# The second MLP's product block is rounded one group later, and the next tokens are transposed through four PSUM banks

## The chip, the cores and the metric

The kernel runs on one core of a Trainium2 chip. The metric is the device time of one execution in microseconds (us). Beside it, one profiled execution leaves a trace, which gives the start and length of nearly every instruction on each engine: TensorE (PE, its weight loads apart as PEld), VectorE (DVE), ScalarE (ACT), GpSimd (POOL) and the DMA queue of SyncE (SP).

## What is computed

The reference runs a linear-attention recurrence over 4 x 768 tokens, a mixture of experts over its 3072 output rows, and then a second MLP without experts. The change touches only the last stage:

```
a = x @ w1            # 3072x384 @ 384x1024
b = x @ w2
h = a * b @ w3
return (h @ w_out)    # 1024x384
```

Everything is fp32. The kernel folds `w3 @ w_out` into one matrix W (1024 x 384) early on, so that the last stage is p = (x @ w1) * (x @ w2), then out = p @ W.

## The kernel before

**Stages.** The attention takes the first part of the span and the experts the second. The second MLP (`second_mlp`) begins at about 332 us of the 654.7 us span and runs to its end. It is one program written out in full; each engine takes its instructions in the order in which the Python code issues them (`manual_schedule`), and waits on semaphores where the data or a buffer asks for it.

**Blocks and groups.** The 3072 tokens are taken in 6 blocks j of 512. In a block, the 1024 columns of p are taken in 8 groups f of 128, each a [128 x 512] piece: 128 columns of p by 512 tokens. Only the very first piece (j = 0, f = 0) is made in the plain way (`plain`); the other 47 are made by `group` and `finish`, by a scheme that takes fewer columns through TensorE than the two products made apart. Matmuls run on rounded fp32 operands, a high and a low part each, so every product is three matmuls (high x high, low x high, high x low).

**One group.** `group` issues 27 matmuls (L1195) into three PSUM banks: `xy`, whose left half X is written, copied out and accumulated further three times, and whose right half is Y; `za`; and `zb`. ScalarE copies the half bank X to the SBUF tile `st` three times, in between the products that add to X: L1198 (the first copy, `st[:, 1]`, after the group's first product), L1202 (the second, `st[:, 2]`) and L1212 (the last, `st[:, 0]`, after the group's last product). Each product that adds to X must wait until the copy before it has read X. Each of the tags xy, za and zb has two banks, so a group's banks come free for the group after the next; two more banks belong to `po`, and that makes all eight.

**What follows a group.** `finish` puts the piece together on VectorE: `C[:,0]` = st + za (L1172), `C[:,1]` = st + zb (L1175), `C[:,1]` += Y (L1176), and `p_sb` = `C[:,0]` * `C[:,1]` (L1178). Then p_sb is split: `high_p` rounds it to `ph` on ScalarE (L1134, the cast), and `low_p` makes the rest `pl` = p_sb - ph on VectorE (L1140). In the code before, `group(f)` first calls `finish` for group f-1, then issues its own matmuls and copies, and calls `high_p` for group f-1 just ahead of its own last copy L1212. `low_p` of that piece comes in the next `finish`, behind its first instruction.

**End of a block.** After group 7, `finish(True)`, `high_p` and `low_p` make the last piece. `outp(j, m)` for m = 0, 1, 2 then issues 24 matmuls each (L1233) over all eight pieces into a bank `po`, ScalarE copies it to `ob` and a DMA writes it out. Ahead of m = 1 the next block's tokens are transposed: `trans_b` for t = 0 to 3, three transposes each on TensorE (L1106) into one bank `pT` of tag xy (two banks), and a copy to `XA` on ScalarE (L1108). Then XA is split and summed for the next block.

In block 0, groups 1 to 6 also round one sixth of W each (`split_w`: a cast W_hi of 128 x 512 on ScalarE and a subtraction W_lo on POOL, L1222), called as `between`.

Of the kernel before, what the change touches and what calls it, by code (L numbers as in the profile page):

```python
# [8 lines left out]
F32 = mybir.dt.float32  # L9
F32R = mybir.dt.float32r  # L10
# [8 lines left out]
P = 128  # L19
NB, NH, NS, HD = 4, 8, 768, 48  # L20
D = NH * HD
# [6 lines left out]
NF = FF // P  # L28
ND = D // P
# [29 lines left out]
def fused_kernel(ctx, tc, att, kv, wt, u, wg, we, w3, wo, w12, r, k, v, wu, out):  # L59
    nc = tc.nc  # L60
# [164 lines left out]
    with tc.manual_schedule():  # L225
# [21 lines left out]
        zb = con.tile([P, DQ], BF16, name="zb")  # L247
# [41 lines left out]
        for i in range(6):  # L289
            wn = pw[:, i - 1] if i else wc  # L290
            n = 1 << i
# [615 lines left out]
    with tc.manual_schedule():  # L907
# [128 lines left out]
        for s in range(NP + 2):  # L1036
            e, f = divmod(s, NF)
# [41 lines left out]
    def second_mlp(first=None):  # L1079
        bctx = ExitStack()  # L1080
        Bc = bctx.enter_context
        bk = Bc(tc.tile_pool(name="bk", bufs=2, reuse_waits="tile"))
        pb_a = Bc(tc.tile_pool(name="pb_a", bufs=2, space=PSUM, reuse_waits="tile"))
        pb_o = Bc(tc.tile_pool(name="pb_o", bufs=2, space=PSUM, reuse_waits="tile"))
        HB = 256
        with tc.manual_schedule():
            xb, pq, last, low, W_ = {}, {}, [], [], []
            def load_b(j):
                for t in range(4):
                    xb[j, t] = bk.tile([P, D], F32, name="x1", bufs=4)  # L1090
                    r0 = 512 * j + P * t
                    nc.sync.dma_start(out=xb[j, t], in_=xm[r0:r0 + P, :])
# [6 lines left out]
            def by_half(x):  # L1099
                return x[:, 0:2 * ND].rearrange("p (h k) n -> p h k n", h=2)  # L1100

            def trans_b(j, t):
                x1 = xb.pop((j, t))
                pT = pb_a.tile([P, 512], F32, tag="xy", name="pT")[:, 0:D].rearrange("p (k t) -> p k t", k=ND)
                for k in range(ND):
                    nc.tensor.transpose(pT[:, k], x1[:, P * k:P * k + P], ident)  # L1106
                h, o = t // 2, P * (t % 2)
                nc.scalar.copy(out=XA[:, ND * h:ND * h + ND, o:o + P], in_=pT)  # L1108

            def sums_x():  # L1110

                a21, a22, a11, a12 = (XA[:, i] for i in (0, 1, 3, 4))
                s1, s2, s3, s4 = (XA[:, i] for i in range(6, 10))
                for o, a, b, op in ((s1, a21, a22, ALU.add), (s2, s1, a11, ALU.subtract),
                                    (s3, a11, a21, ALU.subtract), (s4, a12, s2, ALU.subtract)):
                    nc.vector.tensor_tensor(out=o, in0=a, in1=b, op=op)

            def high_x(c):
                nc.scalar.copy(out=xh[:, c], in_=XA[:, c])

            def low_x(c):
                nc.vector.tensor_tensor(out=xl[:, c], in0=XA[:, c], in1=xh[:, c].bitcast(F32), op=ALU.subtract)
# [3 lines left out]
            def weights(f, i):  # L1126
                return [w[:, P * i:P * i + P] for w in w12_[f]]

            def tiles():
                return bk.tile([P, 2, 512], F32, name="C"), bk.tile([P, 512], F32, name="p_sb")  # L1130

            def high_p(f, p_sb):
                pq[f] = [bk.tile([P, 512], F32R, name=n, bufs=NF) for n in ("ph", "pl")]
                nc.scalar.copy(out=pq[f][0], in_=p_sb)  # L1134
                low.append((f, p_sb))

            def low_p():
                while low:
                    f, p_sb = low.pop(0)
                    nc.vector.tensor_tensor(out=pq[f][1], in0=p_sb, in1=pq[f][0].bitcast(F32), op=ALU.subtract)  # L1140

            def plain(f):

                C, p_sb = tiles()
                for m, tag in enumerate(("za", "zb")):
                    q = pb_a.tile([P, 512], F32, tag=tag, name=tag)
                    mms = []
                    for k in range(ND):
                        w_hi, w_lo = b12 if k < m else weights(f, 1 + k + 2 * m)
                        for a, b in ((w_hi, xh), (w_lo, xh), (w_hi, xl)):  # L1150
                            mms.append((a, by_half(b)[:, :, k]))
                    if m == 0:

                        mms = [x for i, x in enumerate(mms) if i % 3 < 2] + mms[2::3]
                    for i, (a, b) in enumerate(mms):
                        nc.tensor.matmul(q, a, b, start=(i == 0), stop=(i == 8))
                    if m == 0:
                        nc.scalar.copy(out=C[:, 0], in_=q)
                    else:
                        nc.vector.tensor_tensor(out=p_sb, in0=q, in1=C[:, 0], op=ALU.mult)  # L1160
                high_p(f, p_sb)

            def finish(end=False):

                if not last:
                    return None
                f, C, st, za, zb, Y, p_sb = last.pop()

                def halves(x):
                    return x.rearrange("p (h n) -> p h n", h=2)  # L1170

                nc.vector.tensor_tensor(out=halves(C[:, 0]), in0=st[:, 0:2], in1=halves(za), op=ALU.add)  # L1172
                if not end:
                    low_p()
                nc.vector.tensor_tensor(out=halves(C[:, 1]), in0=st[:, 0:3:2], in1=halves(zb), op=ALU.add)  # L1175
                nc.vector.tensor_tensor(out=halves(C[:, 1]), in0=halves(C[:, 1]),  # L1176
                                        in1=Y[:, None, :].to_broadcast([P, 2, HB]), op=ALU.add)
                nc.vector.tensor_tensor(out=p_sb, in0=C[:, 0], in1=C[:, 1], op=ALU.mult)  # L1178
                if end:
                    low_p()  # L1180
                return f, p_sb

            def group(f, between=None):

                p_last = finish()
                xy, za, zb = (pb_a.tile([P, 512], F32, tag=t, name=t) for t in ("xy", "za", "zb"))
                X, Y = xy[:, 0:HB], xy[:, HB:512]
                C, p_sb = tiles()
                st = bk.tile([P, 3, HB], F32, name="st")

                def mm(o, w, x, first=False):
                    w_hi, w_lo = weights(f, w)
                    for i, (a, b) in enumerate(((w_hi, xh), (w_lo, xh), (w_hi, xl))):
                        m = by_half(b)[:, :, ND - 1] if x is None else b[:, x]
                        nc.tensor.matmul(o, a, m, start=first and i == 0, stop=(i == 2), skip_group_check=True)  # L1195

                mm(X, 1, 3, True)
                nc.scalar.copy(out=st[:, 1], in_=X)  # L1198
                mm(za, 3, None, True)
                mm(za[:, HB:512], 2, 4)  # L1200
                mm(X, 6, 7)
                nc.scalar.copy(out=st[:, 2], in_=X)  # L1202
                mm(zb, 5, None, True)
                mm(zb[:, HB:512], 4, 9)
                mm(za[:, 0:HB], 8, 1)
                mm(Y, 0, 6)
                mm(X, 7, 8)
                if between:
                    between()
                if p_last:  # L1210
                    high_p(*p_last)
                nc.scalar.copy(out=st[:, 0], in_=X)  # L1212
                last.append((f, C, st, za, zb, Y, p_sb))

            def split_w(i):
                if i == 0:
                    W_.extend(late.tile([P, NF, D], F32R, name=n) for n in ("W_hi", "W_lo"))
                m, h = divmod(i, 2)
                c = slice(P * m, P * m + P)
                g = slice(h * NF // 2, (h + 1) * NF // 2)  # L1220
                nc.scalar.copy(out=W_[0][:, g, c], in_=W[:, g, c])
                nc.gpsimd.tensor_tensor(out=W_[1][:, g, c], in0=W[:, g, c], in1=W_[0][:, g, c].bitcast(F32),  # L1222
                                        op=ALU.subtract)
# [45 lines left out]
            for j in range(NBLK):  # L1269
                if 0 < j < NBLK - 1:  # L1270
                    load_b(j + 1)
                for f in range(NF):
                    if j + f == 0:
                        plain(f)
                    else:
                        group(f, (lambda: split_w(f - 1)) if j == 0 and f <= 2 * ND else None)
                high_p(*finish(True))
                low_p()
                for m in range(ND):
                    if j + 1 < NBLK and m == 1:  # L1280
                        for t in range(4):
                            trans_b(j + 1, t)
                        high_x(slice(1, 2 * ND))
                        low_x(slice(1, 2 * ND))
                        sums_x()
                        high_x(SUMS)
                        low_x(SUMS)
                    outp(j, m)
# [178 lines left out]
```

## Time and profile before

| what | value |
|---|---|
| device time, 3 runs | 656.81 us median (656.54 to 657.01) |
| device time of the profiled execution | 656.39 us |
| its span, first to last instruction | 654.7 us |
| mean granted TensorE clock | 0.996 of full speed |
| busy in the span: PE, PEld, DVE, ACT, POOL | 622.8, 546.4, 470.6, 290.5, 143.4 us |
| span of the 8 groups of the second block (j = 1) | 33.08 us |
| span of its first `outp` with the transposes behind it | 7.98 us (422.74 to 430.72) |

The device time is 1.7 us longer than the span, which holds only what lies between the first and the last instruction. Busy times of PE count a matmul from its start to its modelled end, and the ends of successive matmuls overlap, so on PE the starts of successive matmuls tell more than the busy share.

### The profile page before, as it was taken

The page shows a single profiled execution, that of the slowest core. Times are in us where ns is not written, and L with a number is a line of the kernel's source. Part 1 is how long each engine was busy: PE and PEld are TensorE (multiplying, and loading weights), DVE is VectorE, ACT ScalarE, POOL GpSimd, SP SyncE. Part 2 cuts the span into 40 slices and gives each one's busy share as a digit, 9 for nine tenths or more (in the row PEclk, how much of TensorE's full clock was granted, in tenths as well). Part 3 has the DMA queues.
Part 4 walks back from the last instruction along what each step waited for, and adds up shares of the span by engine and source line. Part 5 has one row for each costly group of instructions (what it writes and reads, how often), then busy time and mean ns, then how long its engine had stood idle before and what let it go on. Part 6 is the DMA issues. An engine that isn't in the chain of part 4 may idle for free.

```text
span 654.7 us, 15181 instructions
## 1 busy us (share of the span) xinstructions
PE 622.8 (95%) x6289; PEld 546.4 (83%) x6289; DVE 470.6 (72%) x820; ACT 290.5 (44%) x704; POOL 143.4 (22%) x140
## 2 busy tenths in 40 slices
PE   7989999999999999999988999999999999999996
PEld 6978888887699999999967789879879878878884
DVE  6699999984687999999657727745754763754770
ACT  2565565444265666765444333333333333342330
POOL 4855556451221223241232100000000000000000
PEclk9899999999999999999999999999999999999999
DMA  8889987674188768775220011002002002000001
GB/s 308 349 292 362 333 295 251 234 242 135 38 286 276 266 238 300 246 283 164 68 68 0 1 60 38 0 34 65 2 32 65 1 17 80 2 18 32 1 2 53
DMA packets 26798, 90.60 MB, mean 138 GB/s; under 512 B 4010, under 2 KB 10299, under 8 KB 25697
## 3 DMA queue, kind: packets, MB, share of 16 engines
q1 hardware_dynamic: 24672, 84.11, 36.7%
q0 software_dynamic: 2048, 5.44, 2.5%
q8 instruction: 51, 0.84, 0.5%
q14 instruction: 27, 0.21, 0.1%
HBM read 77.81 MB, written 12.58 MB: 138 GB/s over the span
## 4 chain that ended last, share of the span: by engine, by line
PE 46%; DVE 36%; issue 7%; ACT 6%; DMA 4%; SPq 0%; POOL 0%; DVEq 0%; ACTq 0%
PE po L1233 11%; PE hp L922 5%; PE y L941 5%; DVE p_sb L1178 5%; PE wp L707 5%; DVE C L1176 4%; DVE C L1172 4%; DVE C L1175 4%; DVE pl L1140 4%; DMA TB<-in_att 3%; DVE elo L86 3%; PE xy L1195 2%; PE sc L370 2%; ACT st L1212 2%; PE za L1195 2%
## 5 line engine op out<-in xcount | busy, mean ns | idle before, releaser
L1172 DVE TENSOR_TENSOR C<-st,za 128x512 f32<-128x512 f32 x47 | 32.4, 689 | 84.6 <-ACT st L1212 84.6
L1134 ACT CAST ph<-p_sb 128x512 fp32r<-128x512 f32 x48 | 29.8, 621 | 97.9 <-DVE p_sb L1178 96.5
L1195 PE MATMUL xy<-bxh,w12h 128*128 128x256 f32 x188 | 56.2, 299 | 8.1 <-ACT st L1198 8.1
L86 DVE TENSOR_TENSOR elo<-raw,ehi 128x768 fp32r<-128x768 f32 x64 | 60.5, 951 | 3.9 <-ACT ehi L85 3.6
L1233 PE MATMUL po<-pl,W_hi 128*128 128x512 f32 x144 | 57.2, 398 | 1.8 <-DVE pl L1140 1.8
L922 PE MATMUL hp<-xh,ehi 128*128 128x256 f32 x192 | 55.3, 290 | 2.2 <-DVE hl L926 1.5
L1233 PE MATMUL po<-ph,W_hi 128*128 128x512 f32 x144 | 56.6, 393 | 0.0
L1233 PE MATMUL po<-ph,W_lo 128*128 128x512 f32 x144 | 56.1, 390 | 0.0
L85 ACT CAST ehi<-raw 128x768 fp32r<-128x768 f32 x64 | 52.6, 828 | 1.9 <-DMA raw<-in_we 1.9
L922 PE MATMUL hp<-xh,elo 128*128 128x256 f32 x192 | 53.3, 279 | 0.0
L922 PE MATMUL hp<-xl,ehi 128*128 128x256 f32 x192 | 53.3, 279 | 0.0
L1195 PE MATMUL xy<-bxh,w12l 128*128 128x256 f32 x188 | 53.0, 282 | 0.0
L1195 PE MATMUL xy<-bxl,w12h 128*128 128x256 f32 x188 | 53.0, 282 | 0.0
L707 PE MATMUL wp<-wo_s,w 128*128 128x384 f32 x128 | 50.4, 505 | 0.0
L404 ACT ACTIVATE zv<-KV,z 128x48 f32<-128x48 f32 x184 | 44.0, 324 | 11.9 <-DVE z L394 7.8
L1195 PEld LDWEIGHTS xy<-bxh,w12h 128*128 128x128 f32 x188 | 35.8, 190 | 13.7 <-ACT st L1198 13.4
L1195 PE MATMUL za<-bxh,w12l 128*128 128x512 f32 x141 | 45.2, 320 | 0.0
L1195 PE MATMUL za<-bxh,w12h 128*128 128x512 f32 x141 | 45.0, 319 | 0.0
L1195 PE MATMUL za<-bxl,w12h 128*128 128x512 f32 x141 | 44.7, 317 | 0.0
L941 PE MATMUL y<-ehi,hh 128*128 128x384 f32 x128 | 43.4, 339 | 0.0
L941 PE MATMUL y<-ehi,hl 128*128 128x384 f32 x128 | 43.2, 337 | 0.0
L941 PE MATMUL y<-elo,hh 128*128 128x384 f32 x128 | 43.1, 336 | 0.0
(249 smaller groups left out, 1659.3 us busy)
## 6 DMA issues: line engine op xcount, KB each, us to landing
raw<-in_we SPq DMA_DIRECT2D x32, 768.0 KB, 5.2
KV<-in_kv SPq DMA_DIRECT2D x24, 576.0 KB, 6.2
TB<-in_att SPq DMA_DIRECT2D x24, 512.0 KB, 6.3
raww<-in_w SPq DMA_DIRECT2D x8, 1024.0 KB, 7.9
raw<-in_w SPq DMA_DIRECT2D x8, 768.0 KB, 6.5
xm<-xg SPq DMA_DIRECT2D x48, 96.0 KB, 3.8
out<-ob SPq DMA_DIRECT2D x18, 256.0 KB, 2.0
x<-xm SPq DMA_DIRECT2D x20, 192.0 KB, 2.5
```

Of the source, the lines that this page charges most:

```text
L85: nc.scalar.copy(out=hi, in_=raw)
L86: (eng or nc.vector).tensor_tensor(out=lo, in0=raw, in1=hi.bitcast(F32), op=ALU.subtract)
L404: nc.scalar.activation(out=zv[:, h], in_=v[:, h], func=AF.Copy, scale=z[:, h:h + 1])
L707: nc.tensor.matmul(ps, w3[:, g], wo_s[:, g], start=(g == 0), stop=(g == NF - 1))
L922: nc.tensor.matmul(hp, a, b, start=(i == 0), stop=(i == 8))
L941: nc.tensor.matmul(ys[e, t], a[:, P * t:P * t + P], b[:, D:2 * D], start=(f == 0 and i == 0), stop=(f == NF - 1 and i == 2))
L1134: nc.scalar.copy(out=pq[f][0], in_=p_sb)
L1140: nc.vector.tensor_tensor(out=pq[f][1], in0=p_sb, in1=pq[f][0].bitcast(F32), op=ALU.subtract)
L1172: nc.vector.tensor_tensor(out=halves(C[:, 0]), in0=st[:, 0:2], in1=halves(za), op=ALU.add)
L1178: nc.vector.tensor_tensor(out=p_sb, in0=C[:, 0], in1=C[:, 1], op=ALU.mult)
L1195: nc.tensor.matmul(o, a, m, start=first and i == 0, stop=(i == 2), skip_group_check=True)
L1233: nc.tensor.matmul(po, a[:, f, c], b, start=(i == 0), stop=(i == 3 * NF - 1))
```

## The change

The rounding of a piece moves. In the code before, piece f-1 was put together and rounded within group f, the cast being issued ahead of group f's last copy. Now `group(f)` issues its first product and its first copy (L1196 in the new numbering), then calls `high_p`, which casts whatever waits in the new list `high`: that is the piece of group f-2. After it, `finish` puts together piece f-1 and leaves it in `high`. So the cast of a piece comes one group later. Within `finish`, `low_p` now always stands behind the second addition. `split_w` moves with it, from behind the group's last product to behind the cast. `C` gets one buffer where it had two. At a block's end, cast and `finish` are called twice, to drain two pieces. Apart from that, the transposes of the next block go through the banks of tags za and zb in turn, four banks in all, where before they had the two of tag xy. The numbers and shapes of all instructions stay the same.

```diff
-                pT = pb_a.tile([P, 512], F32, tag="xy", name="pT")[:, 0:D].rearrange("p (k t) -> p k t", k=ND)
+                pT = pb_a.tile([P, 512], F32, tag=("za", "zb")[t % 2], name="pT")[:, 0:D].rearrange("p (k t) -> p k t", k=ND)
...
-                return bk.tile([P, 2, 512], F32, name="C"), bk.tile([P, 512], F32, name="p_sb")
-
-            def high_p(f, p_sb):
-                pq[f] = [bk.tile([P, 512], F32R, name=n, bufs=NF) for n in ("ph", "pl")]
-                nc.scalar.copy(out=pq[f][0], in_=p_sb)
-                low.append((f, p_sb))
+                return bk.tile([P, 2, 512], F32, name="C", bufs=1), bk.tile([P, 512], F32, name="p_sb")
+
+            def high_p():
+                while high:
+                    f, p_sb = high.pop(0)
+                    pq[f] = [bk.tile([P, 512], F32R, name=n, bufs=NF) for n in ("ph", "pl")]
+                    nc.scalar.copy(out=pq[f][0], in_=p_sb)
+                    low.append((f, p_sb))
...
-                f, C, st, za, zb, Y, p_sb = last.pop()
+                f, st, za, zb, Y = last.pop()
+                C, p_sb = tiles()
...
                 nc.vector.tensor_tensor(out=halves(C[:, 0]), in0=st[:, 0:2], in1=halves(za), op=ALU.add)
-                if not end:
-                    low_p()
                 nc.vector.tensor_tensor(out=halves(C[:, 1]), in0=st[:, 0:3:2], in1=halves(zb), op=ALU.add)
+                low_p()
                 nc.vector.tensor_tensor(out=halves(C[:, 1]), in0=halves(C[:, 1]),
                                         in1=Y[:, None, :].to_broadcast([P, 2, HB]), op=ALU.add)
                 nc.vector.tensor_tensor(out=p_sb, in0=C[:, 0], in1=C[:, 1], op=ALU.mult)
-                if end:
-                    low_p()
-                return f, p_sb
+                high.append((f, p_sb))
 
             def group(f, between=None):
 
-                p_last = finish()
...
                 mm(X, 1, 3, True)
                 nc.scalar.copy(out=st[:, 1], in_=X)
+                high_p()
+                finish()
+                if between:
+                    between()
                 mm(za, 3, None, True)
...
                 mm(X, 7, 8)
-                if between:
-                    between()
-                if p_last:
-                    high_p(*p_last)
                 nc.scalar.copy(out=st[:, 0], in_=X)
...
-                high_p(*finish(True))
+                for _ in range(2):
+                    high_p()
+                    finish()
                 low_p()
```

The first place is ScalarE's order in the middle of the third block (j = 2). Before, from the last copy of group 2 to that of group 4; `p_sb_6261` is the piece of group 2 and `st_6306` belongs to group 3:

```order
L1212 COPY st_6262<-xy_6257 128x256
L1198 COPY st_6306<-xy_6301 128x256
L1202 COPY st_6306<-xy_6301 128x256
L1134 CAST ph_6336<-p_sb_6261 128x512
L1212 COPY st_6306<-xy_6301 128x256
L1198 COPY st_6350<-xy_6345 128x256
L1202 COPY st_6350<-xy_6345 128x256
L1134 CAST ph_6380<-p_sb_6305 128x512
L1212 COPY st_6350<-xy_6345 128x256
```

The same place after the change; `st_6294` belongs to group 3, and `p_sb_6259` is the piece of group 1:

```order
L1210 COPY st_6250<-xy_6247 128x256
L1196 COPY st_6294<-xy_6291 128x256
L1136 CAST ph_6299<-p_sb_6259 128x512
L1204 COPY st_6294<-xy_6291 128x256
L1210 COPY st_6294<-xy_6291 128x256
L1196 COPY st_6338<-xy_6335 128x256
L1136 CAST ph_6343<-p_sb_6303 128x512
L1204 COPY st_6338<-xy_6335 128x256
L1210 COPY st_6338<-xy_6335 128x256
```

The cast has moved from just ahead of the group's last copy to just behind its first, and within group 3 it takes the piece of group 1 where it took that of group 2.

The second place is VectorE's order at the end of the second block (j = 1): the pieces of groups 6 and 7. Before, with `st_5966` of group 6 and `st_6010` of group 7:

```order
L1172 TENSOR_TENSOR C_5964<-st_5966,za_5962 128x512
L1140 TENSOR_TENSOR pl_5997<-p_sb_5921,ph_5996 128x512
L1175 TENSOR_TENSOR C_5964<-st_5966,zb_5963 128x512
L1176 TENSOR_TENSOR C_5964<-C_5964,xy_5961 128x512
L1178 TENSOR_TENSOR p_sb_5965<-C_5964 128x512
L1172 TENSOR_TENSOR C_6008<-st_6010,za_6006 128x512
L1175 TENSOR_TENSOR C_6008<-st_6010,zb_6007 128x512
L1176 TENSOR_TENSOR C_6008<-C_6008,xy_6005 128x512
L1178 TENSOR_TENSOR p_sb_6009<-C_6008 128x512
L1140 TENSOR_TENSOR pl_6041<-p_sb_5965,ph_6040 128x512
L1140 TENSOR_TENSOR pl_6050<-p_sb_6009,ph_6049 128x512
```

After the change, with `st_5954` of group 6 and `st_5998` of group 7:

```order
L1175 TENSOR_TENSOR C_6006<-st_5954,za_5952 128x512
L1176 TENSOR_TENSOR C_6006<-st_5954,zb_5953 128x512
L1142 TENSOR_TENSOR pl_6004<-p_sb_5963,ph_6003 128x512
L1178 TENSOR_TENSOR C_6006<-C_6006,xy_5951 128x512
L1180 TENSOR_TENSOR p_sb_6007<-C_6006 128x512
L1175 TENSOR_TENSOR C_6042<-st_5998,za_5996 128x512
L1176 TENSOR_TENSOR C_6042<-st_5998,zb_5997 128x512
L1142 TENSOR_TENSOR pl_6040<-p_sb_6007,ph_6039 128x512
L1178 TENSOR_TENSOR C_6042<-C_6042,xy_5995 128x512
L1180 TENSOR_TENSOR p_sb_6043<-C_6042 128x512
L1142 TENSOR_TENSOR pl_6050<-p_sb_6043,ph_6049 128x512
```

The subtraction `pl` now stands between the two instructions that both write `C[:,1]`, and at the end of the block one subtraction, not two, is left behind the last product.

## Rows read from the trace of the kernel before

**Rows 1.** The waits of the whole span: us in total, times, longest.
```profile
ACT ph L1134 <- DVE p_sb L1178: 96.5, 47, 3.2
DVE C L1172 <- ACT st L1212: 84.6, 47, 8.1
...
PE xy L1195 <- ACT st L1198: 8.1, 26, 0.9
```

**Rows 2.** Busy us by stretch: length, PE, PEld, DVE, ACT, POOL, clock, DMA.
```profile
338.14:370.69 32.55, 28.79 (x191) 25.76 (x189) 22.76 (x32) 13.29 (x33) 7.77 (x6) 1.00 0.04 12
389.66:422.74 33.08, 32.22 (x217) 29.32 (x216) 21.73 (x34) 11.78 (x30) 0.00 (x0) 1.00 0.10 32
598.24:631.33 33.09, 32.22 (x218) 29.32 (x216) 21.75 (x34) 11.78 (x30) 0.00 (x0) 1.00 0.03 9
441.72:449.50 7.78, 7.78 (x56) 7.26 (x55) 2.67 (x4) 2.79 (x7) 0.00 (x0) 1.00 0.42 135
436.28:441.72 5.44, 5.44 (x26) 4.50 (x24) 1.23 (x1) 1.05 (x2) 0.00 (x0) 1.00 0.13 50
474.79:480.86 6.07, 5.84 (x26) 4.33 (x25) 4.49 (x7) 1.51 (x3) 0.00 (x0) 1.00 0.00 0
480.86:482.76 1.90, 1.50 (x13) 1.18 (x12) 0.00 (x0) 1.45 (x4) 0.00 (x0) 1.00 0.13 50
```

**Rows 3.** Timeline of a later group, third block: start, us, engine, instruction, [idle before].
```profile
463.19 0.69 DVE L1172 TENSOR_TENSOR C<-st,za 128x512 f32<-128x512 f32 x1 [0.96 <-ACT st L1212]
463.49 0.39 PE L1195 MATMUL xy<-bxh,w12h 128*128 128x256 f32 x1 [0.21 <-ACT st L1198]
463.80 0.68 DVE L1140 TENSOR_TENSOR pl<-p_sb,ph 128x512 fp32r<-128x512 f32 x1
464.40 0.68 DVE L1175 TENSOR_TENSOR C<-st,zb 128x512 f32<-128x512 f32 x1
465.18 0.69 DVE L1176 TENSOR_TENSOR C<-C,xy 128x512 f32<-128x512 f32 x1
465.91 0.69 DVE L1178 TENSOR_TENSOR p_sb<-C 128x512 f32<-128x512 f32 x1
466.63 0.62 ACT L1134 CAST ph<-p_sb 128x512 fp32r<-128x512 f32 x1 [2.12 <-DVE p_sb L1178]
467.56 0.69 DVE L1172 TENSOR_TENSOR C<-st,za 128x512 f32<-128x512 f32 x1 [0.96 <-ACT st L1212]
```

**Rows 4.** Timeline where the block's second group begins, third block.
```profile
445.60 0.28 PE L1195 MATMUL xy<-bxh,w12h 128*128 128x256 f32 x1
445.80 0.37 ACT L1212 COPY st<-xy 128x256 f32<-128x256 f32 x1 [1.75 <-PE xy L1195]
446.16 0.37 ACT L1198 COPY st<-xy 128x256 f32<-128x256 f32 x1
446.21 0.69 DVE L1172 TENSOR_TENSOR C<-st,za 128x512 f32<-128x512 f32 x1 [8.10 <-ACT st L1212]
447.57 0.37 ACT L1202 COPY st<-xy 128x256 f32<-128x256 f32 x1 [1.03 <-PE xy L1195]
```

**Rows 5.** Timeline of that block's end, in its first output and transposes.
```profile
478.39 0.69 DVE L1178 TENSOR_TENSOR p_sb<-C 128x512 f32<-128x512 f32 x1
...
479.00 1.46 DVE L1140 TENSOR_TENSOR pl<-p_sb,ph 128x512 fp32r<-128x512 f32 x2
...
479.74 0.50 PE L1233 MATMUL po<-pl,W_hi 128*128 128x512 f32 x1 [0.23 <-DVE pl L1140]
480.08 0.39 PE L1233 MATMUL po<-ph,W_hi 128*128 128x512 f32 x1
...
482.08 0.93 PE L1106 MATMUL pT<-ident,x 128*128 128x128 f32 x6 [0.40 <-ACT XA L1108]
```

**Rows 6.** Timeline in the first block: POOL's piece of W and VectorE's product.
```profile
350.84 1.30 POOL L1222 TENSOR_TENSOR W_lo<-W,W_hi 128x512 fp32r<-128x512 f32 x1 [3.43 <-ACT W_hi L1221]
...
351.63 1.06 DVE L1178 TENSOR_TENSOR p_sb<-C 128x512 f32<-128x512 f32 x1
```

More of the change, by code (lines that the diff above doesn't have):

```diff
@@ L1086, in second_mlp @@
         with tc.manual_schedule():
-            xb, pq, last, low, W_ = {}, {}, [], [], []
+            xb, pq, last, high, low, W_ = {}, {}, [], [], [], []
             def load_b(j):
@@ L1160, in plain, with finish @@
                         nc.vector.tensor_tensor(out=p_sb, in0=q, in1=C[:, 0], op=ALU.mult)
-                high_p(f, p_sb)
-            def finish(end=False):
+                high.append((f, p_sb))
+            def finish():
                 if not last:
-                    return None
-                f, C, st, za, zb, Y, p_sb = last.pop()
+                    return
+                f, st, za, zb, Y = last.pop()
+                C, p_sb = tiles()
                 def halves(x):
@@ L1178, in finish @@
                 nc.vector.tensor_tensor(out=p_sb, in0=C[:, 0], in1=C[:, 1], op=ALU.mult)
-                if end:
-                    low_p()
-                return f, p_sb
+                high.append((f, p_sb))
             def group(f, between=None):
-                p_last = finish()
                 xy, za, zb = (pb_a.tile([P, 512], F32, tag=t, name=t) for t in ("xy", "za", "zb"))
                 X, Y = xy[:, 0:HB], xy[:, HB:512]
-                C, p_sb = tiles()
                 st = bk.tile([P, 3, HB], F32, name="st")
@@ L1207, in group @@
                 mm(X, 7, 8)
-                if between:
-                    between()
-                if p_last:
-                    high_p(*p_last)
                 nc.scalar.copy(out=st[:, 0], in_=X)
-                last.append((f, C, st, za, zb, Y, p_sb))
+                last.append((f, st, za, zb, Y))
             def split_w(i):
```

## The prediction

> **What bounds the kernel now.** I read the list of waits first. Three entries belong together [rows 1]: ScalarE's cast waits for VectorE's product p_sb, 47 times; VectorE's first addition waits for ScalarE's last copy, 47 times; and TensorE waits for ScalarE's first copy, 26 times. The first two need not matter, as neither engine has to be full. The third is the engine that all else feeds.
>
> The stretches, cut at TensorE's starts, size it [rows 2]. The 8 groups of a block take 33.08 us in the second block and 33.09 in the sixth; the three between look the same. But a block's first two groups take 7.78, or 3.89 each, with PE busy for all of it. Eight at that pace are 31.12. A block thus loses 1.96 us in its later groups, and block 0, with 32.55 for 7 groups, loses 32.55 - 27.23 = 5.32. The granted clock is 1.00 in all of them.
>
> The timeline of a later group says why [rows 3]. VectorE's first addition starts at 463.19, its product at 465.91, the cast at 466.63 once that is done, the group's last copy behind the cast, and the next group's first addition at 467.56. That is a ring, 4.37 us around: last copy, first addition, pl, two more additions, product, cast, next last copy. Each instruction in it waits for the one before, and as ScalarE takes its work in order, the next group's first copy stands behind that last copy, and TensorE's second product into X waits for it (463.49, 0.21 us idle after the modelled end of the matmul before). The ring is longer than TensorE's 3.89, so it sets the pace of every later group.
>
> **The group loop after the change.** The cast leaves this place. Behind a group's first copy it now takes the piece of two groups ago, so the last copy waits for TensorE alone. I lay out the new group from T, the start of its first matmul, by the unstalled group boundary [rows 4], T = 445.60: last copy of the group before at T+0.20, first copy at T+0.56, VectorE's first addition at T+0.61, second copy at T+1.97 when X is ready. The cast can start by the end of the first copy, T+0.93, and is done by T+1.55 (0.62 [rows 3]), ahead of the second copy. VectorE's spacings come from [rows 3]: 0.60 between instructions that don't need each other (463.80 to 464.40), 0.73 from third addition to product, 0.69 for the last. In the new order pl stands between the two instructions on `C[:,1]`, so it fills the 0.78 that the dependent pair took (464.40 to 465.18). So: addition T+0.61, second addition 1.21, pl 1.81 (its cast is done at 1.55), third addition 2.41, product 3.14, end 3.83. The next group starts at T+3.89, and the cast of this piece is due at T+3.89+0.93 = 4.82: it finds its input with 0.99 us to spare. VectorE has work for 3.22 of 3.89 us. The bank xy is wanted again at T+3.89 and its last reader, the third addition, ends at 3.10. Nothing in this layout makes TensorE wait. The ring still exists, but it now spans two groups: 0.41 from last copy to addition, 3.22 through VectorE, 0.03 to the cast, 0.53 to the second copy (cast at 466.63, its follower's addition 0.40 behind at 467.56), about 1 us through that copy and TensorE's last product; 5.2 in all, 2.6 a group.
>
> So each group takes 3.89: 5 x 1.96 + 5.32 = **15.1 us** less.
>
> **split_w** is issued earlier, its cast behind the piece's cast, done by T+2.17; the second copy slips 0.2 and TensorE needs it read only when its last product begins, three matmuls before T+3.89, or T+3.46 by the mean of 0.144 (54 in 7.78 us). It costs nothing. POOL's W_lo then runs at about T+2.2 to 3.5. In the trace, W_lo at 350.84 for 1.30 went with a product of 1.06 where it takes 0.69 otherwise [rows 6, 3]: the product ended 0.55 after POOL did. Laid on the new order, that is an end at 4.05 rather than 3.83, still 0.77 ahead of the cast. The 0.37 was in the ring before (part of block 0's larger loss); now it lies in slack. The Trainium skill, SBUF — State Buffer, "Who interferes with whom", states it harder: a VectorE instruction with two SBUF inputs and a POOL instruction that reads SBUF exclude each other for the whole instruction, whoever comes first. By it pl holds POOL off to 2.50, POOL then holds the product off to 3.80, and it ends at 4.49, still ahead of 4.82; the sum is the same either way. If that cover were gone, 0.37 in each of five groups is 1.9 us.
>
> **The end of a block.** The first output's 24 matmuls take 6.07 us, an undisturbed output's 5.44 [rows 2]; TensorE waits for the last pl twice, and the pace after a wait is 0.34 for one matmul, not 0.23 [rows 5]. Before, the product of the last piece came 478.39 - 474.79 = 3.60 after the output's first matmul, and both subtractions behind it, the second ended at 480.46, or 5.67. After: the last copy no longer stands behind the cast of piece 6, so the layout above holds with T at the first output matmul: product at 3.14, cast 0.73 later at 3.87, pl 0.65 behind that at 4.52, end 5.21. The 24th matmul, which needs it, is due at 23 x 5.44/24 = 5.21. I take a rest of 0.2 (a tenth for the signal, a tenth for the slower restart) of the 0.63, so 0.42 saved, at 6 blocks **2.5 us**. Bounds: 0 if the tail slips back, 3.8 if all goes.
>
> **The transposes.** Twelve take 1.90 us to the next output's first matmul; the second six wait 0.40 for ScalarE to empty a bank [rows 2, 5]. From their start at 482.08 to that matmul at 482.76 the second six take 0.68; twice that is 1.36. With four banks nothing is to be emptied first: the readers of za and zb, the first two additions, are done by 1.21 + 0.68 after the output began. So 0.54 less, of which I take 0.5, five times: **2.5 us**. Bound below: 0, if another wait takes its place. What ScalarE and VectorE do with the copies has most of two outputs to hide in.
>
> **The sum.** 15.1 + 2.5 + 2.5 = 20.1. The profiled execution took 656.39 us (span 654.7, 1.7 around it), 0.42 under the median of 656.81. That gives 636.3 from the one and 636.7 from the other; I take **636.4 us**.
>
> **Rivals.**
> - *VectorE becomes the pace.* `C` has one buffer, so each first addition follows the product that reads it, and if all five spacings were the dependent 0.78, a group takes 3.9 to 4.0. For it: VectorE is the next fullest. Against: three of the five don't depend on their neighbour. 0.07 more in 45 groups: 639.6. Chance 0.08.
> - *Only the groups gain.* The last pl comes no sooner or the transposes wait for something else. Against: the layout of the tail. Both gone: 641.4, one gone: 638.9. Chance 0.10.
> - *TensorE is full already.* PE is busy 32.22 of 33.08 us [rows 2], so at most 0.86 a block is to be had, 3.76 in block 0, and some 3 at the ends: 645. Against: a later group takes 4.37 and a first one 3.89, which the busy share hides, as matmuls' modelled ends overlap the wait. The Trainium skill, Perfetto Trace Analysis, "Identifying the Most-Contended Engine", calls matmul busy time a bad measure for this reason and points to weight loads; by their share, 29.32/33.08 against 7.26/7.78, a block would drop to 31.4, 1.7 less, near the 1.96. Chance 0.03.
> - *Block 0 keeps POOL's toll*: 638.3. Chance 0.03.
> - *Slower.* The cast now stands ahead of the second and last copies. If p_sb came late, ScalarE would sit on it with both copies behind, and TensorE would wait at its last product. The second copy must end by T+3.46, so the cast may start as late as 2.5, which p_sb 2.6 later than laid out would bring about. From there the two-group ring sets the pace, and to use up the gain it must grow from 5.2 to over 8.7, twice the 3.89 + 20.1/45. No row of VectorE is near that. A ring of 9.0 would give 4.5 a group and 664. Chance 0.02.
>
> The rest, 0.74, goes to the forecast, by itself 635.0 to 637.8. The range for 8 in 10 takes in the first two rivals' nearer ends and the upper bounds of the ends of blocks: **634.6 to 640.0**. A difference of 0.2% (1.3 us) is about what can be told from none. All cases but the last are faster: **0.96 faster, 0.02 the same, 0.02 slower**.
>
> **What would show it.** Group starts on TensorE 3.89 apart in every block and no entry in which TensorE waits for the first copy; ScalarE's cast with no long wait for p_sb within a block; VectorE's five instructions in 3.2 us; a first output of 5.5 to 5.7 us; twelve transposes in a row, with the next output about 1.4 after their start. It is wrong if the later groups show a new common period, if TensorE waits for xy, or if the clock's row falls below 1.00 in the second MLP, where it now reads 1.00 in stretches with TensorE at work without a gap [rows 2].

## The result and the profile after

The changed kernel takes 635.06 us (median of 4 runs, 634.88 to 639.26) against 656.86 for the kernel before: a ratio of 0.9684, 95% interval 0.9644 to 0.9724. The forecast was 636.4, with a range of 634.6 to 640.0. The profiled execution took 634.88 us, with a span of 633.2, so the span fell by 21.5. Medians below are those of the fast runs; the one slow run on record, of e1 (859.45 us at a granted clock of 0.65), is left out.

The list of waits after the change, from the first group to the end: us in total, times, longest. It answers to [rows 1].

```profile
ACT st L1210 <- PE xy L1193: 81.8, 47, 1.8
DVE C L1175 <- ACT st L1210: 69.5, 46, 7.8
...
ACT ph L1136 <- DVE p_sb L1180: 16.5, 6, 2.8
...
PEld po L1231 <- DVE pl L1142: 1.6, 6, 0.3
ACT ph L1136 <- DVE p_sb L1162: 0.6, 1, 0.6
...
PEld xy L1193 <- DVE C L1178: 0.2, 1, 0.2
```

Of the three linked entries one is left, and it no longer closes a loop. VectorE's first addition still waits for the last copy, 46 times, but that copy (now L1210) waits for TensorE and for nothing else, 47 times. The cast waits for the product 6 times, once at each block's end, and once more for the very first piece (0.6 us, L1162), not 47 times. TensorE no longer waits for the first copy at all; what is left there is 1.6 us on pl at six block ends and one wait of 0.2 for the bank xy.

The same stretches as in [rows 2], after the change; the columns are length, busy us of PE, PEld, DVE, ACT and POOL, the granted clock and two columns on DMA:

```profile
338.04:365.51 27.47, 27.47 (x190) 25.48 (x189) 22.96 (x32) 13.60 (x33) 8.85 (x6) 1.00 0.04 12
383.34:414.48 31.14, 31.14 (x217) 29.06 (x216) 21.73 (x34) 12.18 (x30) 0.00 (x0) 1.00 0.11 34
579.15:610.29 31.14, 31.14 (x217) 29.06 (x216) 21.74 (x34) 12.18 (x30) 0.00 (x0) 1.00 0.03 9
365.51:371.10 5.59, 5.59 (x27) 4.41 (x25) 3.87 (x6) 1.51 (x3) 0.00 (x0) 1.00 0.00 0
371.10:372.33 1.23, 1.23 (x14) 1.23 (x12) 0.00 (x0) 1.03 (x3) 0.00 (x0) 1.00 0.00 0
```

Eight groups of a block take 31.14 us, 3.89 each, with PE busy throughout; block 0's seven take 27.47. A block's first output takes 5.59, and from the first transpose to the next output's first matmul it is 1.23. Added up, the 21.5 us are: 5.08 in block 0's groups, 5 x 1.94 = 9.70 in the others', 3.26 at the block ends (0.48 at five, 0.86 at the one that had a longer wait before), 5 x 0.68 = 3.40 in the transposes, and 0.1 ahead of the second MLP.

The timeline where the third group of the third block begins, VectorE and ScalarE (start, us, instruction, idle time before):

```profile
440.29 0.37 ACT L1210 COPY st<-xy 128x256 f32<-128x256 f32 x1 [1.75 <-PE xy L1193]
440.70 0.37 ACT L1196 COPY st<-xy 128x256 f32<-128x256 f32 x1
440.97 0.62 ACT L1136 CAST ph<-p_sb 128x512 fp32r<-128x512 f32 x1
442.06 0.37 ACT L1204 COPY st<-xy 128x256 f32<-128x256 f32 x1 [0.47 <-PE xy L1193]
```

```profile
440.70 0.69 DVE L1175 TENSOR_TENSOR C<-st,za 128x512 f32<-128x512 f32 x1 [1.09 <-ACT st L1210]
441.31 0.68 DVE L1176 TENSOR_TENSOR C<-st,zb 128x512 f32<-128x512 f32 x1
441.90 0.69 DVE L1142 TENSOR_TENSOR pl<-p_sb,ph 128x512 fp32r<-128x512 f32 x1
442.50 0.68 DVE L1178 TENSOR_TENSOR C<-C,xy 128x512 f32<-128x512 f32 x1
443.22 0.69 DVE L1180 TENSOR_TENSOR p_sb<-C 128x512 f32<-128x512 f32 x1
```

The group's first matmul is at T = 440.09 (the last copy stands 0.20 behind it, as in [rows 4]). The layout had the additions at T+0.61, 1.21 and 2.41, pl at 1.81 and the product at 3.14; here they are at 0.61, 1.22, 2.41, 1.81 and 3.13. The cast stands directly behind the first copy and waits for nothing.

### The profile page after: what moved, and what is told of

Read it like the earlier page. It is cut to its first block, busy times and chain, and to the rows that moved or that the text cites. A ratio compares the mean times of both kernels' runs of the same rounds, so it can differ in the third digit from the quotient of the medians.

```text
span 633.2 us, 15204 instructions
## 1 busy us (share of the span) xinstructions
PE 614.4 (97%) x6289; PEld 546.4 (86%) x6289; DVE 467.0 (74%) x820; ACT 292.4 (46%) x704; POOL 143.9 (23%) x140
## 4 chain that ended last, share of the span: by engine, by line
PE 77%; DVE 13%; DMA 4%; issue 3%; ACT 1%; POOL 1%; SPq 0%; DVEq 0%; ACTq 0%; POOLq 0%
PE po L1231 16%; PE xy L1193 11%; PE za L1193 10%; PE zb L1193 8%; PE hp L922 7%; PE y L941 6%; PE wp L707 5%; PE sc L370 2%; DVE elo L86 2%; DMA TB<-in_att 2%; PE S L440 2%; DVE hl L926 1%; PE G L427 1%; PE y L424 1%; PE y L427 1%
## 5 line engine op out<-in xcount | busy, mean ns | idle before, releaser
L1210 ACT COPY st<-xy 128x256 f32<-128x256 f32 x47 | 17.6, 374 | 81.8 <-PE xy L1193 81.8
L1193 PE MATMUL xy<-bxh,w12h 128*128 128x256 f32 x188 | 53.3, 283 | 0.0
L959 POOL DMA_INDIRECT xm<-yo,sidx x16 | 23.8, 1485 | 89.5 <-DVE yo L956 75.4
```

What stands on the lines that cost most here:

```text
L959: ins = nc.gpsimd.indirect_dma_start(out=xm[:, :], out_offset=bass.IndirectOffsetOnAxis(ap=sidx[:, j, 1:2], axis=0), in_=yo, in_offset=Non ...
```

## The experiments

The start of the second MLP differs by up to 5 us between profiled executions (last section), so I compare stretches of the profiled execution, from TensorE's starts. "Second MLP" is from its first group's first matmul to the end of the span; "block 0" its seven groups, "later" the eight groups of the other blocks, "first output" that of a block with transposes behind it, "transposes" from the first transpose to the next matmul. Each is the usual value of the blocks; single first outputs are up to 0.4 longer, and one row of transposes in e11 is 1.2 longer.

| kernel | median | second MLP | block 0 | later | first output | transposes |
|---|---|---|---|---|---|---|
| before | 656.86 | 316.56 | 32.55 | 33.08 | 6.07 | 1.91 |
| after | 635.06 | 295.16 | 27.47 | 31.14 | 5.59 | 1.23 |
| e1 after, one tag | 642.42 | 298.49 | 27.48 | 31.14 | 5.59 | 1.91 |
| e2 before, four banks | 653.28 | 313.09 | 32.51 | 33.08 | 6.06 | 1.23 |
| e3 after, cast ahead of last copy | 648.84 | 308.83 | 32.28 | 32.10 | 6.28 | 1.23 |
| e4 before, cast behind last copy | 648.21 | 304.73 | 31.17 | 31.77 | 5.47 | 1.91 |
| e5 before, pl later | 650.75 | 311.08 | 32.58 | 32.10 | 5.86 | 1.91 |
| e6 after, two C | 635.66 | 295.40 | 27.48 | 31.14 | 5.59 | 1.23 |
| e7 after, one more addition | 644.58 | 304.71 | 32.19 | 31.14 | 6.30 | 1.23 |
| e8 before, one more addition | 683.20 | 341.61 | 33.53 | 36.54 | 7.25 | 1.91 |
| e9 before, no W_lo | 655.40 | 314.30 | 30.37 | 33.08 | 6.06 | 1.91 |
| e10 after, one more, no W_lo | 639.62 | 299.53 | 27.25 | 31.14 | 6.31 | 1.23 |
| e11 after, two more additions | 673.16 | 330.17 | 32.24 | 34.02 | 7.82 | 1.23 |
| e12 after, pl of piece 6 last | 634.43 | 294.43 | 27.48 | 31.14 | 5.47 | 1.23 |

**The two parts apart.**

```diff
e1, on after:   tag=("za", "zb")[t % 2]  ->  tag="xy"
e2, on before:  tag="xy"  ->  tag=("za", "zb")[t % 2]
```

e1: 

> The changed kernel with the next tokens' transposes back on the two xy banks; all else as changed. Theory: the four banks are worth 0.68 us at each of five blocks, by themselves, so 635.1 + 3.4 = 638.5 us, with the second six transposes waiting 0.4 us for ScalarE again and the groups at 31.1 us a block. Rival, the transposes were hidden and the whole gain is the cast's: 635.1.

e2: 

> The kernel before with the transposes alone moved to za and zb in turn. Theory: 656.9 - 3.4 = 653.5 us, groups of a block still 33.1. Rival, the four banks only pay once the groups run free (here za and zb are read later, behind the late last copy): 656 to 657.

The second MLP got 3.33 longer in e1 and 3.47 shorter in e2, and in both only the column of the transposes moved. So the two parts of the change add up and don't need each other: 3.4 us are the banks', and the rest comes with the rounding that was moved. The median of e1 is 3.9 above the expectation, but its profiled execution entered the second MLP at 342.21 and not 338.04.

**The ring.**

```diff
e3, on after, in group:
                 nc.scalar.copy(out=st[:, 1], in_=X)
-                high_p()
                 finish()
...
+                high_p()
                 nc.scalar.copy(out=st[:, 0], in_=X)
```

> The changed kernel with the cast put back ahead of the group's last copy, where it takes the piece that this group has just finished; finish, pl's place, one C and the transposes stay as changed. Theory of the ring: it closes again over one group, 0.40 + 0.60 + 0.60 + 0.60 + 0.72 + 0.72 + 0.53 = 4.17 us around, shorter than the old 4.37 because pl fills the dependent gap; some 0.8 us a block in five blocks, 2 in the first, 0.4 at six block ends: 643.5 (641 to 646), with TensorE waiting for the first copy again. Rival, that the gain came from finish being issued behind the first copy and not from the cast: 635.1.

```diff
e4, on before, in group:
-                if p_last:
-                    high_p(*p_last)
                 nc.scalar.copy(out=st[:, 0], in_=X)
+                if p_last:
+                    high_p(*p_last)
```

> The kernel before with two lines exchanged: the cast of the piece of group f-1 stands behind group f's last copy and not ahead of it. Theory of the ring: the last copy no longer waits for VectorE, so the ring is open although the cast comes no group later; but the cast now sits between last copy and next first copy, which then ends at about T+1.45 where TensorE wants it at 1.40, so some 0.1 us a group is left: 3.95 to 4.0 a group, 643 us in all. Rival, that a whole group of delay is needed because the product is never ready in time: the first copy takes over the wait and the pace stays at 4.37, 656 to 657.

```diff
e5, on before, in finish:
-                if not end:
-                    low_p()
                 nc.vector.tensor_tensor(out=halves(C[:, 1]), in0=st[:, 0:3:2], in1=halves(zb), op=ALU.add)
+                if not end:
+                    low_p()
```

> The kernel before with pl moved on VectorE from behind the first addition to behind the second (within a block; the block's end as before). Theory of the ring: the ring loses the dependent gap, 0.78 to 0.60, so 4.18 around instead of 4.37; 6 rounds of it a block, 1.1 us in each of six blocks and 0.2 at each end: 649 us. Rival, VectorE's order is off the path: 656.9.

e3 puts the cast back and keeps all else, and the ring is back: the cast waits for the product 47 times, 95.2 us in all, and a later block takes 32.10. That is also what e5 takes, in which the old ring is shortened by the same 0.18 that pl fills. Within a later block's groups VectorE and ScalarE execute the same order of instructions in e3 and e5, so the two are one test and not two; that they agree to 0.01 says that what still differs (where the code calls `finish`, the buffers of C) costs nothing there. With `finish` and pl as changed, the cast's place decides 0.96 us a later block (32.10 against 31.14); pl's place, with the cast as before, gives 0.98 (e5). The cast's new place with pl's old one was not run.

The starts of successive groups on TensorE show the pace itself. Late in a block they come 4.36 us apart before, 4.17 in e3 and e5 (4.17 and 4.18 expected), 4.00 in e4 (3.95 to 4.0 expected) and 3.89 after. The ring takes hold late: before, a block's first four groups take 3.89 to 3.95 each and only the last four 4.36, which is why a block loses 1.96 and not eight times 0.47.

e4 shows that the delay of a whole group isn't what opens the ring in the later blocks: exchanging two lines gives 1.31 of the 1.94 us there, and leaves what the cast then costs ahead of the first copy, 0.08 a group, about as expected. The place behind the first copy, which takes a piece finished a group earlier, gives the rest. Block 0 came out otherwise than expected: it gained nothing in e5, where 1.1 was expected, and lost 4.8 in e3, where 2 was (e3's first outputs lost 0.7, where 0.4 was); in e4 it gained 1.4, against 5.1 in the full change.

**What VectorE can still take.**

```diff
e6, on after:   name="C", bufs=1  ->  name="C", bufs=2
e7, on after, e8, on before, in finish:
+                nc.vector.tensor_tensor(out=halves(p_sb), in0=st[:, 0:2], in1=halves(za), op=ALU.add)
                 nc.vector.tensor_tensor(out=p_sb, in0=C[:, 0], in1=C[:, 1], op=ALU.mult)
e11: as e7, and the same line once more behind the first addition
```

e6: 

> The changed kernel with two buffers of C, as before the change. Theory: VectorE stands idle 0.67 us a group, and the wait of its first addition for the product before is long over: 635.1, no change. Rival, the one buffer costs VectorE a turn-around that reaches TensorE: faster by 1 us or more.

e7: 

> The changed kernel with one more VectorE addition of 128x512 in every finish (the first addition once more, into p_sb, which the product then overwrites). Theory: 3.22 + 0.60 = 3.82 of VectorE in a group of 3.89, and the product's 0.99 us ahead of its cast take the 0.6: the groups stay at 31.1 us a block; only at six block ends, where pl of the last piece is the last thing, 0.65 shows: 639.0 us. Rival, VectorE sets the pace already: 0.6 in 45 groups, 662 or more.

e8: 

> The kernel before with the same extra addition in every finish. Theory of the ring: 0.6 to 0.7 longer around, about 5.0; 6 rounds of it a block are 3.9 us, and some 1.3 at each block's end: 656.9 + 31 = 688 us (680 to 692). Rival, VectorE is idle for a quarter of the stage and the addition is hidden: 657 to 661.

e11: 

> The changed kernel with two more VectorE additions in every finish. Theory: 3.22 + 0.60 + 0.60 = 4.4 or a little more is over TensorE's 3.89, so VectorE sets the pace and TensorE waits for the bank xy: 31.14 a block becomes 33 to 34.5, the first output 7 to 8, block 0 about 36; 668 us (655 to 675). Rival, that one more buffer of delay still hides it: within 4 us of the run with one extra addition, 645 to 649.

e6 changes no stretch up to the last output by more than 0.01 (the 0.24 in its second MLP lie behind the last block's groups): the one buffer of C costs nothing. The same addition costs 0.00 us in a later block of the changed kernel (e7) and 3.46 in one of the kernel before (e8, 3.9 expected). VectorE executes as many instructions of the same shapes in both; what differs is that in one they lie in slack and in the other in the ring, whose groups come 4.96 us apart in e8 where they came 4.36 apart. With two (e11) the slack is used up, the groups come 4.51 apart with VectorE at work without a gap, and a block takes 2.88 more. At the block ends e7 pays 0.7, as expected, and 1.0 at two of them. What was not expected is block 0 in e7, 4.7 us longer. The timeline there, POOL and VectorE:

```profile
353.54 1.29 POOL L1221 TENSOR_TENSOR W_lo<-W,W_hi 128x512 fp32r<-128x512 f32 x1 [3.73 <-ACT W_hi L1220]
```

```profile
352.39 0.69 DVE L1175 TENSOR_TENSOR C<-st,za 128x512 f32<-128x512 f32 x1
353.00 0.68 DVE L1176 TENSOR_TENSOR C<-st,zb 128x512 f32<-128x512 f32 x1
353.59 1.78 DVE L1142 TENSOR_TENSOR pl<-p_sb,ph 128x512 fp32r<-128x512 f32 x1
355.30 0.68 DVE L1178 TENSOR_TENSOR C<-C,xy 128x512 f32<-128x512 f32 x1
355.90 0.68 DVE L1180 TENSOR_TENSOR p_sb<-st,za 128x512 f32<-128x512 f32 x1
356.61 0.69 DVE L1181 TENSOR_TENSOR p_sb<-C 128x512 f32<-128x512 f32 x1
357.40 0.69 DVE L1175 TENSOR_TENSOR C<-st,za 128x512 f32<-128x512 f32 x1
```

pl, issued 0.05 behind W_lo, lasts 1.78 us and not 0.69, and ends 0.54 behind W_lo's end: it is held off while POOL subtracts. VectorE's round is then 352.39 to 357.40, 5.01 us with no idle time, above TensorE's 3.89, and TensorE waits for the bank xy (3.5 us in five waits of its weight loads). In e11 the further addition delays pl by 0.6 and its wait shrinks to 0.5, so block 0 hardly changes (32.24, where about 36 was expected).

**Block 0's own ring.**

```diff
e9, on before, e10, on e7, in split_w:
-                nc.gpsimd.tensor_tensor(out=W_[1][:, g, c], in0=W[:, g, c], in1=W_[0][:, g, c].bitcast(F32),
-                                        op=ALU.subtract)
+                nc.gpsimd.memset(W_[1][:, g, c].bitcast(F32), 0.0)
```

e9: 

> The kernel before, with POOL's six subtractions W_lo replaced by six settings of W_lo to zero, which read nothing: the low part of W is left out of the result. By the traces so far block 0 has a ring of its own, through ScalarE's W_hi, POOL's W_lo and VectorE's product, which can't run beside W_lo. Theory: without it block 0 falls back to the ring of the other blocks, 4.37 in five groups where it took 4.73: 32.55 becomes 30.7 us, all other stretches as before, 655.0 in all. Rival, block 0 is slower because of ScalarE's extra cast: 32.5.

e10: 

> The changed kernel with one more VectorE addition in every finish, as in the run with the extra addition, and W_lo set to zero instead of subtracted (the low part of W is left out of the result). There block 0 went from 27.5 to 32.2 us. Theory: that was VectorE held up 1.1 us a group by W_lo, and with it away block 0 is back at 27.5 and its first output at 6.3: 639.6 us. Rival, the extra cast W_hi in front of the second copy is what costs: block 0 stays near 32.

Both fell where expected: block 0 takes 30.37 in e9 (30.7 expected) and 27.25 in e10 (27.5), all other stretches unchanged. The extra cast W_hi is still there in both. The settings to zero read nothing and run at 335.65 to 338.52 in e9, ahead of the groups, so they neither wait for W_hi nor hold up the product; the two links are taken away at once. So before the change block 0's groups did not run in the ring of [rows 3] but, from the third on, in a second one beside it: second copy, W_hi, W_lo, then the product that W_lo holds up, cast, last copy, first copy, TensorE's second product into X, second copy, 4.73 us around (TensorE's wait there ends at 349.21 and at 353.94). That is why e5 gained nothing there: it shortened the ring that was not the longer one. In e3, W_lo holds up pl: there pl lasts 1.48 us in block 0 and not 0.69, and the groups come 4.96 apart, the ring's 4.17 and that 0.79.

Part of block 0's loss is no ring. Before, `plain` ended with `high_p(f, p_sb)`; after, it ends with `high.append((f, p_sb))`, a line that the diff ahead of the prediction leaves out. So before the change ScalarE waited for the very first product, with the cast of that piece ahead of group 1's first copy, and TensorE waited for the copy:

```profile
339.65 0.62 ACT L1134 CAST ph<-p_sb 128x512 fp32r<-128x512 f32 x1 [1.41 <-DVE p_sb L1160]
340.17 0.37 ACT L1198 COPY st<-xy 128x256 f32<-128x256 f32 x1
340.59 0.39 PE L1195 MATMUL xy<-bxh,w12h 128*128 128x256 f32 x1 [0.89 <-ACT st L1198]
```

Group 2 then started 5.04 us behind group 1, 1.15 over the pace of 3.89; after the change it starts 3.89 behind, with the first copy at 338.59. So of block 0's 5.32 us, 1.15 were this wait, and nearly all the rest five groups at 4.73. No run changed this line alone.

**A block's end with one subtraction moved back.**

```diff
e12, on after, in the last finish of a block:
-                low_p()
                 nc.vector.tensor_tensor(out=halves(C[:, 1]), in0=halves(C[:, 1]),
                                         in1=Y[:, None, :].to_broadcast([P, 2, HB]), op=ALU.add)
                 nc.vector.tensor_tensor(out=p_sb, in0=C[:, 0], in1=C[:, 1], op=ALU.mult)
+                low_p()
```

> The changed kernel with one more edit: in the last finish of a block, pl of piece 6 stands behind the product of piece 7 and not ahead of the third addition, as it did before the change. Theory: the product of the last piece starts 0.4 us sooner, pl of piece 7 ends at about 4.8 after the output's first matmul and the 24th matmul no longer waits: first outputs 5.47 instead of 5.59, 0.12 at six places, 634.4 against 635.1 (too little for the whole runs to tell, but the stretches of the profile will). Rival, the wait of the 24th matmul was not on pl: 5.59 stays.

The block end of e4 had pointed to it: with pl of piece 6 behind the last product the first output took 5.47 there. e12's stretches, the first output and a later block:

```profile
369.75:375.22 5.47, 5.47 (x26) 4.46 (x25) 3.96 (x6) 1.51 (x3) 0.00 (x0) 1.00 0.00 0
387.46:418.60 31.14, 31.14 (x217) 29.05 (x216) 21.73 (x34) 12.17 (x30) 0.00 (x0) 1.00 0.11 34
```

The wait of the 24th matmul is gone and all else is as in the changed kernel: 0.12 us at five places and 0.18 in the last block, 0.73 in the second MLP. The whole runs (634.43, ratio 0.9648 with 0.9626 to 0.9670) can't tell this from the changed kernel's by themselves.

## Why the prediction was right

The sum was 20.1 us less, and the span fell by 21.5. The three terms were off by -0.3, +0.8 and +0.9, and 0.1 came ahead of the second MLP; so the span fell by 1.4 more than the sum, and the result lies near the lower end of the range.

- **The ring and the group loop, 15.1 us less.** Measured 14.8 (9.70 + 5.08). For the later blocks the mechanism is shown by e3, e4, e5 and e8, each with the pace that its ring gives, and the new layout held to 0.01 us. The ring did not set the pace of every later group, as I wrote, but only from the fifth on; the sum took the measured 33.08 and did not depend on it. For block 0 the size was right and the reason was not: I took all of its 5.32 to be this ring, and it was a second ring through W_lo and the first piece's cast. That the same change takes those away too was in part luck. Block 0 kept 0.24 of its 5.32, at one place: the first matmul of its third group came at 345.96 and not 345.82, waiting for the bank xy, and the restart took the rest. That is one of the signs of being wrong that I had named, once and for 0.2 us. My layout has a piece's cast ahead of W_hi in every group, but in the second group of block 0 none was due, so W_lo started at 343.46, T+1.53 and not T+2.2, and pl behind it took 1.57.
- **W_lo lies in slack.** That part of the sum was right, the figure behind it was not. Laid out from [rows 6], the product would end at T+4.05. Block 0 of the changed kernel, POOL and VectorE in the group with T = 353.83:

```profile
355.93 1.55 POOL L1220 TENSOR_TENSOR W_lo<-W,W_hi 128x512 fp32r<-128x512 f32 x1 [2.35 <-ACT W_hi L1219]
```

```profile
355.64 0.69 DVE L1142 TENSOR_TENSOR pl<-p_sb,ph 128x512 fp32r<-128x512 f32 x1
356.25 0.68 DVE L1178 TENSOR_TENSOR C<-C,xy 128x512 f32<-128x512 f32 x1
356.96 1.07 DVE L1180 TENSOR_TENSOR p_sb<-C 128x512 f32<-128x512 f32 x1
```

  pl came first, and W_lo lasts 1.55 instead of 1.29; then the product lasts 1.07 instead of 0.69 and ends at 358.03, T+4.20, as it does in the groups before and behind. Against the cast due at T+4.82 the slack left was 0.62, not 0.77, and e7 shows what happens when it is used up. I had also put block 0's 0.37 down to the ring of [rows 3]; e9 shows a ring of its own. The estimate by the rule of the Trainium skill, SBUF — State Buffer, "Who interferes with whom", was T+4.49. The trace agrees with that rule in that either engine holds the other off, whichever came first, but the estimate is 0.29 too late: if the one held off then takes its usual time, it goes on some 0.14 us ahead of the other's recorded end, here and in e7.
- **The block ends, 2.5.** Measured 3.26. In the third block the first output matmul starts at 463.45 and the last product at 466.58, 3.13 behind it and as laid out (3.14); the rest left of the wait is 0.15, where I took 0.2. The larger part of the difference, 0.38, is the one block whose longer wait I had left out of the sum.
- **The transposes, 2.5.** Measured 3.4, the term furthest off: 0.68 a block, where I took 0.5 of a worked-out 0.54. I doubled the second six's 0.68, but those six had themselves started out of a wait; twelve without one take 1.23, not 1.36.
- **The rivals.** VectorE as the pace: refuted by e6 and e7 for the blocks from the second on, and near in block 0. Only the groups gain: refuted, as the first output fell by 0.48 and the transposes by 0.68 (e1 and e2 for the transposes alone). TensorE full already: a block gained 1.94, not the 0.86 of the busy share. The estimate by weight loads, the measure of the Trainium skill (Perfetto Trace Analysis, "Identifying the Most-Contended Engine"), was 1.7. Block 0 keeps POOL's toll: it kept 0.24 us, not 1.9. The cast in front of the copies: within a block it waited once, 0.6 us for the very first piece; the second copy behind it came later, at 340.63, but TensorE did not wait for it.

## What to carry to other kernels

Where two engines each wait for the other as many times as there are loop turns, follow one turn round by its starts: if it comes back to the same instruction, and is longer than what the fullest engine needs for a turn, its length is the pace, whatever the engines' busy shares say. Moving one instruction out of the way opens it: by a turn, or, for two thirds of a later block's gain here, behind the copy that others wait for. What work costs is then read from its place: the same addition cost 0.6 us a group in a ring (4.96 against 4.36) and nothing beside one. And look for a second ring just below the first, and for the tail behind the loop: both decide what a half measure brings.

## What was not expected of the hardware

The granted clock of TensorE falls in the first stage, at a place that differs by execution (once in most profiled executions, twice in e9's). With it the start of the second MLP differs by up to 5 us, 337.72 in e5 to 342.77 in e4, between kernels that are the same up to there. The stretches of the changed kernel show it early, after PE was busy for 2.16 of 4 us:

```profile
12.00:16.00 4.00, 2.16 (x48) 1.65 (x47) 3.57 (x7) 1.91 (x8) 3.92 (x4) 1.00 1.01 416
16.00:20.00 4.00, 4.00 (x69) 3.73 (x66) 2.71 (x4) 2.27 (x9) 2.73 (x3) 0.57 1.03 419
20.00:24.00 4.00, 4.00 (x130) 3.75 (x130) 1.02 (x2) 3.67 (x12) 3.78 (x8) 1.00 1.02 415
```

In e12's profiled execution it kept 1.00 there and fell later:

```profile
32.00:40.00 8.00, 6.45 (x168) 5.78 (x163) 7.97 (x10) 3.64 (x12) 3.88 (x5) 1.00 0.76 262
40.00:44.00 4.00, 3.25 (x88) 3.26 (x89) 3.97 (x6) 3.45 (x11) 2.92 (x3) 0.81 0.96 325
44.00:48.00 4.00, 4.00 (x26) 3.30 (x25) 3.97 (x7) 1.46 (x3) 1.57 (x2) 0.50 0.90 309
48.00:52.00 4.00, 4.00 (x61) 2.92 (x62) 4.00 (x4) 2.81 (x11) 2.30 (x2) 0.50 0.89 310
```

0.50 is the lower level, 1.2 of 2.4 GHz. Ahead of it PE was busy for 6.45 of 8 us. Here the second MLP began at 342.27 and not 338.04. The profiled executions of e1, e4, e8 and e11, which began it at 342.2 to 342.8, all have a mean of 0.87 from 20 to 60 us, where the changed kernel's has 1.00. In e2 it fell later still, at 56 to 64 us. What decides between the places was not tried.
